# Dummy matmuls between the first transposes of a gated MLP kernel on one core

## The chip, the cores and the metric

The kernel runs on one core of a Trainium2 chip. The metric is the device time of one execution in microseconds (us). An execution that leaves a profile also has a span, from its first to its last instruction; the time is about 1.8 us more than the span (before: 544.01 us and 542.2 us for the same execution). Engines are called PE (matrix engine), DVE and ACT (vector and scalar), POOL, and SP, which issues transfers here.

## The reference

```python
# x: 2048 x 1024, w_gate and w_up: 1024 x 3584, w_down: 3584 x 1024, all bf16
g = einsum("bsd,df->bsf", x, w_gate)
u = einsum("bsd,df->bsf", x, w_up)
h = gelu_tanh(g) * u
return einsum("bsf,fd->bsd", h, w_down)
```

## The kernel before

The kernel is a tuned one; almost all of it is a dense stream of matmuls. Only its opening matters here. The first 512 rows of x arrive as four tiles of 128 rows. PE turns each tile by eight transposes (matmuls against an identity), DVE or ACT copies the result to SBUF, and then the first real matmuls run. Ahead of the transposes stand five dummy matmuls with zeros, to raise the clock of PE.

```python
NWARM = 5
...
warm = xpool.tile([P, N], bf16, name="warm")        # N = 512, P = 128
nc.vector.memset(warm, 0.0)
...
def turn(xT, xn, c, i, copy):                        # one row tile
    tp = bank[4 + i].bitcast(bf16).rearrange("p (k r) -> p k r", k=NKB)
    for ko in range(NKB):                            # NKB = 8
        nc.tensor.transpose(tp[:, ko, :], xn[i][:, ko * P : (ko + 1) * P], ident)
    copy(out=xT[c][:, :, i * P : (i + 1) * P], in_=tp)
...
xT = new_x()
xn0 = load_x(0)                                      # four transfers, x tiles 0 to 3
for k0, k1 in ((0, 2), (2, 5), (5, NKB)):
    load_wf(nc.sync, k0, k1)                         # first weight tile, gate and up
for ko in range(KH):
    transposing(xT, 1, ko, N)                        # second block of x
w = load_w(1)                                        # second weight tile, gate and up
...
for _ in range(NWARM):
    nc.tensor.matmul(bank[3], lhsT=warm[:, :P], rhs=warm, start=True, stop=True)
for i in range(NS):                                  # NS = 4
    turn(xT, xn0, 0, i, on_act if i == 1 else on_dve)
plain(bank[0:4], 0, range(0, 2), parts=2)            # 16 real matmuls of 256 columns
plain(bank[0:4], 0, range(2, NKB))                   # 24 of 512 columns
...
plain(bank[4:8], 1, range(KH))
...
nxt = {"p1": first_product(odd, xT, w)}              # needs the second weight tile
```

## Time and profile before

| | before |
|---|---|
| time, three executions | 542.15, 542.86, 543.13 us |
| the profiled execution: time, span | 544.01, 542.2 us |
| PE busy | 534.2 us, 99% of the span |
| half-rate stretch at the start | to about 10.3 us |

The first lines of the page, busy time and share of the span by engine:

```profile
span 542.2 us, 7385 instructions
## 1 busy us (share of the span) xinstructions
PE 534.2 (99%) x2371; PEld 379.3 (70%) x2405; DVE 341.0 (63%) x524; ACT 258.2 (48%) x463; POOL 238.9 (44%) x217
```

PE is the bound. The timeline of PE from 3 to 12 us, with start and length in us, the count after the x, and in brackets how long PE was idle before and what ended it:

```profile
2.44 1.06 PE L502 MATMUL bank<-warm 128*128 128x512 bf16 x2
3.63 1.89 PE L448 MATMUL bank<-ident,xn 128*128 128x128 bf16 x16
6.61 1.89 PE L448 MATMUL bank<-ident,xn 128*128 128x128 bf16 x16 [1.08 <-DMA xn<-in_x_dram]
8.29 3.96 PE L111 MATMUL bank<-xT,w 128*128 128x256 bf16 x20
```

Sixteen transposes take 1.89 us: one starts every 0.107 us. PE waits 1.08 us for x tile 2, and the first real matmul starts at 8.29 us. Narrower windows of the same timeline give the rate:

```profile
8.72 1.06 PE L111 MATMUL bank<-xT,w 128*128 128x256 bf16 x4
...
10.21 0.86 PE L111 MATMUL bank<-xT,w 128*128 128x256 bf16 x6
```

The last of a group adds its pipeline to the length: (1.06 - 0.42) / 3 = 0.213 us between starts at 9 us, where one such matmul has a length of 0.42. In the second row it is (0.86 - 0.27) / 5 = 0.118 us, with 0.27 the length of one there. So the clock doubles near 10.3 us. (The clock row of the page reads full speed from 0 on, because its first record begins at 10.28 us.)

The chain of waits of the first 25 us, start and length in us:

```profile
1.65 4.91 DMA xn<-in_x_dram
6.56 0.05 issue
6.61 1.89 PE bank L448 x16
8.50 2.68 PE bank L111 x16
11.17 0.05 issue
11.23 10.74 PE bank L111 x49
```

After the landing of x tile 2 the chain never leaves PE.

### The profile page before, as it was taken

What the parts mean: (1) busy time and instruction counts of PE and PEld (TensorE: products, weight loads), DVE (VectorE), ACT (ScalarE), POOL (GpSimd) and SP (SyncE); (2) the same over time, 40 slices, a digit from 0 to 9 for tenths busy, and PEclk for the clock granted to TensorE, in tenths of its full rate; (3) what the DMA queues carried; (4) which work ended last, traced back from release to release, by engine and by line L of the source; (5) the groups of instructions that cost most, each with busy time, mean ns of one, the idle gap of its engine ahead of it and who ended that gap; (6) DMA issues with size and microseconds to landing.
All of it is one profiled execution on the core that took longest, in us unless ns stands there. A gap on an engine that the chain in (4) does not pass through costs nothing.

```text
span 542.2 us, 7385 instructions
## 1 busy us (share of the span) xinstructions
PE 534.2 (99%) x2371; PEld 379.3 (70%) x2405; DVE 341.0 (63%) x524; ACT 258.2 (48%) x463; POOL 238.9 (44%) x217
## 2 busy tenths in 40 slices
PE   8999999999999999999999999999999999999997
PEld 5477777776776646888876677667777775488885
DVE  3796666667666894695945545555544459676730
ACT  2466666655666410165355555555555541114431
POOL 0169976667774500000097777777766600000000
PEclk9999999999999999999999999999999999999999
DMA  8976656667664899979763232232232069463751
GB/s 195 194 193 176 175 175 174 198 196 189 192 196 139 287 354 308 311 178 318 241 183 89 77 79 77 79 79 79 78 95 60 2 185 383 149 234 96 230 188 48
DMA packets 108133, 93.28 MB, mean 172 GB/s; under 512 B 17216, under 2 KB 92992, under 8 KB 108096
## 3 DMA queue, kind: packets, MB, share of 16 engines
q1 hardware_dynamic: 108096, 92.82, 59.3%
q8 instruction: 19, 0.31, 0.3%
q14 instruction: 18, 0.15, 0.1%
HBM read 74.45 MB, written 15.20 MB: 165 GB/s over the span
## 4 chain that ended last, share of the span: by engine, by line
PE 98%; DMA 1%; issue 0%; SPq 0%; ACT 0%
PE bank L111 97%; DMA xn<-in_x_dram 1%; PE bank L448 0%; SPq L441 0%; ACT st L412 0%
## 5 line engine op out<-in xcount | busy, mean ns | idle before, releaser
L93 POOL TENSOR_TENSOR s<-w 128x512 fp32r<-128x512 bf16 x102 | 119.2, 1188 | 155.3 <-PE bank L111 155.3
L111 PE MATMUL bank<-t,s 128*128 128x512 f32 x648 | 157.0, 398 | 0.0
L111 PEld LDWEIGHTS bank<-t,s 128*128 128x128 f32 x648 | 121.7, 188 | 27.7
L107 ACT COPY p<-bank 128x512 f32<-128x512 f32 x124 | 70.3, 590 | 98.0 <-PE bank L111 95.8
L111 PE MATMUL bank<-xT,w 128*128 128x512 bf16 (+1 forms) x476 | 111.4, 379 | 1.9
L90 DVE TENSOR_TENSOR hT<-g,bank 128x512 bf16<-128x512 f32 x112 | 76.7, 686 | 55.4 <-ACT g L179 49.9
L111 PEld LDWEIGHTS <-w 128*128 128x128 bf16 x504 | 45.7, 99 | 59.4 <-issue 13.5
L90 DVE TENSOR_TENSOR sum<-bank,p 128x512 f32<-128x512 f32 x54 | 37.3, 692 | 53.0 <-PE bank L111 50.8
L179 ACT ACTIVATE g<-sum 128x512 f32<-128x512 f32 x81 | 51.4, 634 | 33.6 <-DVE sum L90 32.6
L111 PE MATMUL bank<-q 128*128 128x512 f32 x240 | 58.9, 389 | 0.0
L111 PE MATMUL bank<-t,sa 128*128 128x512 f32 x216 | 58.6, 413 | 0.0
L93 POOL TENSOR_TENSOR s<-w,s 128x512 fp32r<-128x512 bf16 x50 | 57.7, 1172 | 0.0
L93 POOL TENSOR_TENSOR s<-s,w 128x512 fp32r<-128x512 f32 x50 | 57.0, 1161 | 0.0
L111 PE MATMUL bank<-tb,s 128*128 128x512 f32 x216 | 53.3, 389 | 0.0
L111 PEld LDWEIGHTS bank<-q 128*128 128x128 f32 x240 | 45.0, 188 | 9.4
L111 PE MATMUL bank<-raw,hT 128*128 128x512 bf16 x218 | 48.4, 379 | 0.3
L111 PEld LDWEIGHTS bank<-t,sa 128*128 128x128 f32 x216 | 40.7, 188 | 10.6
L111 PEld LDWEIGHTS bank<-tb,s 128*128 128x128 f32 x216 | 40.5, 188 | 8.4
L102 ACT CAST tb<-raw 128x512 fp32r<-128x512 bf16 x28 | 17.3, 626 | 60.6 <-DMA raw<-in_w_down_dram 28.5
L107 ACT COPY u<-bank 128x512 f32<-128x512 f32 x62 | 35.8, 589 | 17.9 <-PE bank L111 17.9
L90 DVE TENSOR_TENSOR bank<-bank,p 128x512 f32<-128x512 f32 x54 | 37.8, 699 | 8.5 <-PE bank L111 5.2
L90 DVE TENSOR_TENSOR q<-hT 128x512 fp32r<-128x512 bf16 x56 | 38.4, 686 | 4.2 <-PE bank L111 4.2
(45 smaller groups left out, 442.4 us busy)
## 6 DMA issues: line engine op xcount, KB each, us to landing
raw<-in_w_down_dram SPq DMA_DIRECT2D x80, 256.0 KB, 4.8
q<-td SPq DMA_DIRECT2D x60, 256.0 KB, 5.0
w<-in_w_gate_dram SPq DMA_DIRECT2D x27, 512.0 KB, 4.5
w<-in_w_up_dram SPq DMA_DIRECT2D x27, 512.0 KB, 6.3
td<-m SPq DMA_DIRECT2D x12, 768.0 KB, 4.5
w<-td SPq DMA_DIRECT2D x6, 1024.0 KB, 9.8
out_dram<-st SPq DMA_DIRECT2D x32, 128.0 KB, 1.7
td<-w SPq DMA_DIRECT2D x2, 768.0 KB, 7.1
```

Of the source, the lines that this page charges most:

```text
L90: nc.vector.tensor_tensor(out=out, in0=a, in1=b, op=op)
L93: nc.gpsimd.tensor_tensor(out=out, in0=a, in1=b, op=op)
L102: nc.scalar.copy(out=t, in_=src)
L107: nc.scalar.copy(out=t, in_=ps)
L111: nc.tensor.matmul(ps, lhsT=lhs, rhs=rhs, start=start, stop=stop, skip_group_check=True)
L179: nc.scalar.activation(g, src, ACT.Gelu_apprx_tanh)
```

## The change

The intent: keep PE busy between the transposes, so that its clock rises earlier. Three dummies of 256 columns go ahead of row tiles 1, 2 and 3.

```diff
-        for _ in range(NWARM):
-            nc.tensor.matmul(bank[3], lhsT=warm[:, :P], rhs=warm, start=True, stop=True)
+        def keep_warm(n, cols):
+            for _ in range(n):
+                nc.tensor.matmul(
+                    bank[3][:, :cols], lhsT=warm[:, :P], rhs=warm[:, :cols], start=True, stop=True
+                )
+
+        keep_warm(NWARM, N)
         for i in range(NS):
+            if i > 0:
+                keep_warm(3, 2 * P)
             turn(xT, xn0, 0, i, on_act if i == 1 else on_dve)
```

## The prediction

> **What bounds the kernel now.** TensorE. The profile's first part has PE busy 534.2 of 542.2 us; the chain that ended last lies to 97.4% on the matmul line. From 11.2 to 538.8 us PE never waits more than 0.07 us at a time. Only the first 11 us can improve.
>
> **The opening, from the timeline in narrow windows.** Five dummies run 1.19 to 3.50 us. Transposes of tiles 0 and 1 run 3.63 to 5.52, PE idles 1.08 us for tile 2 (landed 6.56), transposes of tiles 2 and 3 run 6.61 to 8.50, and the first real matmul starts at 8.29. Up to about 10.2 us the array runs at half rate: matmuls of 512, 256 and 128 columns start every 0.427, 0.213 and 0.107 us; from 10.3 us on every 0.216 (512) and 0.109 us (256). So the clock rises at about 10.3 us, and the real matmuls before it cost about 1 us too much. (The PEclk row, 1.0 all along, hides this.)
>
> The Trainium skill (TensorE: Matmul & The Clock Gate, Part 1) says that full rate is granted after about 3.4 us of sustained activity, in a free-running window. The trace agrees: a window ending at 10.28 would begin at 6.86, in unbroken work; the one before holds the idle microsecond. The same page (Part 4) says that transposes do not count as activity; here the full rate came after only 2 us of matmuls following transposes, so I think they count.
>
> **What the change adds.** Nine matmuls of 256 columns with zeros, three ahead of tiles 1, 2, 3: 0.64 us a group at half rate, 0.33 at full. Nothing else changes. The first two groups run while PE would wait for tile 2 anyway: tile 0 3.63-4.49, dummies to 5.13, tile 1 to 5.98, dummies to 6.62. Tile 2 starts on time at 6.62, without the gap. The third group, in front of tile 3, is on the critical path: +0.64 us at half rate.
>
> **Balance.** If the clock stays low, the first real matmul slips from 8.29 to about 8.97. But PE is now busy without a break from 3.63, so the clock should rise between 6.9 and 8.9 us. In the good case (about 6.9) tiles 2 and 3 finish near 8.0, the first matmuls wait for the up weights (landed 8.17), and the first block of x ends near 15.1 instead of 16.19 us. Then a next wait caps it: the up half of the second weight tile lands at 19.78 us, and its matmuls start at 20.5 now. So at most 0.7 us is kept against this profiled run. Its clock phase looks lucky, though: a full window after 6.6 us ends anywhere from 10.0 to 13.4, and each us costs 0.5. That would explain the spread of 542.15 to 543.13. Against the median the change then gains about 1 us. Later slack (DVE and POOL operands of the first unit are ready 1.4 to 2.6 us early) is enough not to give it back.
>
> **Prediction.** 541.9 us, 80% range 541.1 to 542.9. Faster by over 2%: 0.2%; within 2%: 99.5%; slower: 0.3%.
>
> **What would show it.** No PE gap before tile 2's transposes; 256-column matmuls at 0.109 us from the first real one, or nearly; the first real matmul at 8.0 to 8.5 us; a new PE wait of up to 1 us near 19 us for the up weights; PE without waits after it; span 541.3 to 541.9.
>
> **What would make it wrong.** Zeros or transposes not counting as activity: then the clock still rises near 10.3 us, the first real matmul is at 8.97 and the kernel is 0.3 us slower. Or the weights landing later than in the profile; or a run-to-run spread larger than the effect.

## The result, and the profile after

The changed kernel takes 542.37 us (median of 4 executions, 542.12 to 542.51), the kernel before 542.50 (4 executions, 541.78 to 543.13). The ratio is 0.9997, with a 95% interval from 0.998 to 1.0015: the same. Ratios here are not quite the ratios of the medians quoted.

The two profiles, however, differ by 1.7 us. The first lines of the page after:

```profile
span 540.5 us, 7403 instructions
## 1 busy us (share of the span) xinstructions
PE 533.0 (99%) x2380; PEld 378.3 (70%) x2414; DVE 340.8 (63%) x524; ACT 258.3 (48%) x463; POOL 238.9 (44%) x217
```

The timeline of PE after, 3 to 12 us:

```profile
3.53 0.91 PE L448 MATMUL bank<-ident,xn 128*128 128x128 bf16 x8
4.27 0.49 PE L503 MATMUL bank<-warm 128*128 128x256 bf16 x3
4.60 0.61 PE L448 MATMUL bank<-ident,xn 128*128 128x128 bf16 x8
5.05 0.49 PE L503 MATMUL bank<-warm 128*128 128x256 bf16 x3
6.25 0.62 PE L448 MATMUL bank<-ident,xn 128*128 128x128 bf16 x8 [0.71 <-DMA xn<-in_x_dram]
6.71 0.49 PE L503 MATMUL bank<-warm 128*128 128x256 bf16 x3
7.03 0.61 PE L448 MATMUL bank<-ident,xn 128*128 128x128 bf16 x8
7.48 4.87 PE L111 MATMUL bank<-xT,w 128*128 128x256 bf16 x28
```

The three dummies of the first group already run at full rate ((0.49 - 0.27) / 2 = 0.11 us apart); the first clock record begins at 4.17 us. **The clock rose before the first of the new dummies began, at 4.27 us.** They cannot have caused it, and the difference between the two profiles is no measure of the change. The chain of waits after shows the rest of it, the earlier landing of x tile 2 (6.20 instead of 6.56 us) and the shorter matmuls:

```profile
1.65 4.55 DMA xn<-in_x_dram
6.20 0.05 issue
6.25 0.62 PE bank L448 x8
6.87 0.33 PE bank L503 x3
7.20 0.45 PE bank L448 x8
7.64 1.90 PE bank L111 x16
```

One more reading from the traces: from the first fp32 matmul (26.36 us before, 24.73 after) to the end it is 515.84 and 515.80 us. In the nine further profiles of real kernels below it is 515.67 to 515.96 us. So what separates these kernels happens in the opening, to within 0.3 us, and is kept to the end.

### The profile page after: what moved, and what is told of

The parts are those of the page before. It is cut to its first block, busy times and chain, and to the rows that moved or that the text cites. A ratio compares the mean times of both kernels' runs of the same rounds, so it can differ in the third digit from the quotient of the medians.

```text
span 540.5 us, 7403 instructions
## 1 busy us (share of the span) xinstructions
PE 533.0 (99%) x2380; PEld 378.3 (70%) x2414; DVE 340.8 (63%) x524; ACT 258.3 (48%) x463; POOL 238.9 (44%) x217
## 4 chain that ended last, share of the span: by engine, by line
PE 98%; DMA 1%; issue 0%; SPq 0%; ACT 0%
PE bank L111 98%; DMA xn<-in_x_dram 1%; PE bank L448 0%; SPq L441 0%; ACT st L412 0%; PE bank L503 0%
## 5 line engine op out<-in xcount | busy, mean ns | idle before, releaser
L111 PEld LDWEIGHTS <-w 128*128 128x128 bf16 x504 | 45.1, 98 | 59.1 <-issue 13.4
```

Source lines behind the costliest of these rows:

```text
L111: nc.tensor.matmul(ps, lhsT=lhs, rhs=rhs, start=start, stop=stop, skip_group_check=True)
```

## The experiments

The prediction takes the clock to be decided anew at the end of every window of about 3.4 us; where these windows lie in the kernel (their phase) changes from execution to execution. **Theory "gap"**: idle time while PE waits for x spoils the window in which the clock could rise; the dummies fill it. **Rival "phase"**: only the position of the free-running window decides, and the dummies do nothing.

### e1: many openings in one execution

The clock's window has some phase in each execution, and one profile shows one phase. So 72 openings were put in front of the unchanged kernel, each with its own loads and preceded by an idle stretch that the DVE makes by a long memset. The core of the edit, condensed:

```diff
+def opening(rep, nwarm, groups, only_transposes=False):
+    nc.vector.tensor_copy(out=rseen, in_=bank[3][:, :1])      # waits for PE
+    nc.vector.memset(flat[:, : 18000 + 542 * rep], 0.0)       # idle stretch for PE
+    ... two columns of each x and weight tile, then `warm`, set by DVE: releases loads and dummies
+    ... loads of x and of the first weight tile as in the kernel; dummies(nwarm, 512)
+    for i in range(NS):
+        if i > 0: dummies(groups[i - 1], 256)
+        turn(rx, rxn, 0, i, ...)
+    ... the 40 real matmuls of the first block
+KINDS = [(5, (0,0,0)), (5, (3,3,3)), (5, (3,3,0)), (6, (3,3,0)), (0, (0,0,0)), (0, (0,0,0), True)]
```

> 72 openings in one execution, ahead of the unchanged kernel (the output stays right, the time is meaningless). Each is preceded by 9 to 16 us without work for the tensor engine, so each meets the clock's window at another phase. Six kinds in turn, 12 of each: B as before (5 dummies, no groups), A as after (groups 3,3,3), A2 without the third group (3,3,0), F with a sixth first dummy (6; 3,3,0), N without any dummies, X without dummies but with 72 further transposes of the first tile. GAP theory (the clock rises at the end of the first 3.4 us window that is busy for some share between 62% and 80%; the idle microsecond spoils it for some phases, the dummies fill it): counted from the first dummy, B rises in two groups, about half of its openings at 2.7 to 4.6 us and about half at 8.0 to 9.5 us; A and A2 all at 2.7 to 6.1 us; the opening of A is then shorter than B's by 0.3 to 0.8 us in the mean, by 1.3 to 1.7 us in the phases where B is late and by nothing in the others. PHASE theory (the dummies do nothing, the two profiles only met other phases): B and A have the same mix of early and late rises. X: if transposes count as activity the rise comes while they still run, 2.7 to 6.8 us after the first; if not, only after the matmuls behind them have run for 2 us or more. A minus A2: 0 to 0.15 us, for the weights hide the third group.

Measured, from the release of the first dummy to the start of the last matmul of the first block, and how often the clock rose later than 7 us after that release:

```
kind                 n  mean   lowest-highest  late rises
B  (before)         12  13.58  12.23 - 15.10   4   (9.11 to 9.57 us; mean of these 14.83, of the others 12.95)
A  (after)          12  13.14  12.31 - 13.86   0
A2 (third gone)     12  13.10  12.67 - 13.70   0
F  (sixth, 3,3,0)   12  13.13  12.62 - 13.67   0
N  (no dummies)     12  13.69  13.07 - 15.22   9   (8 of these 7.25 to 7.95, one 10.30)
```

B has late rises and A has none. By itself this does not refute the phase theory, for the phases were not spread evenly: in ten of the 12 B openings the first dummy came 0.73 to 1.19 us into a window of the clock, in A only once near there (1.21 us; otherwise at 0.47 to 0.63 and at 2.41 to 2.57). e5 mends this. The gap theory is right only in part: late rises are a third and not half (the means differ by 0.44 us, within the foretold 0.3 to 0.8), six of B's eight early rises came at 5.75 to 6.02 us, where 2.7 to 4.6 had been foretold, and B when it is early is 0.19 us *faster* than A. Two openings of kind B at the same phase (the window begins 0.91 us before the release of the first dummy) show that the phase alone does not decide, and what does. Windows of 3.41 us on the clock's grid: PE busy with count, granted clock, DMA share, GB/s. First the late one:

```profile
763.59:767.00 3.41, 2.41 (x23) 0.50 0.95 292
767.01:770.42 3.41, 3.41 (x24) 0.50 0.59 165
```

Then the early one:

```profile
913.78:917.19 3.41, 2.91 (x28) 0.50 1.02 316
917.19:920.60 3.41, 3.41 (x30) 1.00 0.55 142
```

And their timelines, late first:

```profile
763.62 1.70 PE L448 MATMUL bank<-ident,xn 128*128 128x128 bf16 x14
766.32 1.89 PE L448 MATMUL bank<-ident,xn 128*128 128x128 bf16 x16 [1.00 <-DMA xn<-in_x_dram]
```

```profile
913.62 1.89 PE L448 MATMUL bank<-ident,xn 128*128 128x128 bf16 x16
916.00 1.62 PE L448 MATMUL bank<-ident,xn 128*128 128x128 bf16 x16 [0.50 <-DMA xn<-in_x_dram]
```

The first of these windows decides: with a wait of 1.00 us it was busy for 2.41 of 3.41 us and the clock stayed; with 0.50 us it was busy for 2.91 and the clock rose. A wait for x costs the clock its rise only when it takes too much of a window.

The clock changes lie on one grid through the whole execution: every stretch at one rate within the openings is 10.24, 13.65 or 17.07 us long, three, four or five times 3.413. I worked out the busy share of each window from the starts of the matmuls (columns over the rate, transposes and zeros counted). Of 138 windows at half rate with any work, the 72 that raised the clock had shares of 0.755 and more; those that did not had 0.763 and less, so the two sets part at about 0.76, with an overlap of 0.008. That is theory **"share"**: a window raises the clock when PE was busy for about 0.76 of it; some 0.8 us of waiting (0.24 of 3.41) does not cost the rise.

Kind X answers whether transposes count. Windows before and after the rise of one opening in which PE had done nothing but transposes:

```profile
135.54:138.95 3.41, 3.41 (x34) 0.50 1.04 322
138.96:142.37 3.41, 3.41 (x64) 1.00 0.54 142
```

```profile
135.27 5.92 PE L506 MATMUL bank<-ident,xn 128*128 128x128 bf16 x72 [13.83 <-DMA xn<-in_x_dram]
```

The rise at 138.95 us lies amid the transposes, and before them PE was idle for 13.8 us. In all 12 openings of X it came 5.57 to 7.26 us after the release, while the first other matmul ran at 10.18 us or later. Transposes count. (Counted from the first transpose, as foretold, it came after 3.06 to 4.88 us, inside the 2.7 to 6.8. In A and A2 the rise was to come at 6.1 us at the latest, and the latest came at 6.31 and 6.33. A minus A2 is 0.04 us, inside the 0 to 0.15, but the two met different phases, so this hardly tells it from nothing.)

### e2, e3, e4: the real kernels again

e2 is the kernel before, e3 the changed one, both without an edit; e4 is before without its five dummies:

```diff
-    NWARM = 5
+    NWARM = 0
```

> The kernel before against itself, as the measure of noise: ratio 1.000. GAP theory: its executions fall into an early and a late kind, about 1.3 to 1.7 us apart (near 541.9 and near 543.5 us). PHASE theory says the same of before, so this run only sets the scale.

> The changed kernel on the same chip. GAP theory: all executions in the early kind, spread under 0.6 us, median 0.2 to 0.8 us below that of before depending on how many of the before executions are late. PHASE theory: the same two kinds and the same spread as before, medians within 0.3 us either way.

> Before without its first five dummies. Both theories: nearly always a late rise (at 9.3 us or later), so all executions in the late kind or later, 543.3 to 545 us; this gives the whole cost of a late clock in the real kernel, 1.3 to 2.5 us over the early kind. If it is no slower than before, the rise of the clock is not what separates the kinds.

Measured: e2 541.92 us (541.68 to 542.15, 5 executions), all early, ratio 0.9995; e3 542.46 (541.69 to 542.81), ratio 1.0004; e4 542.61 (542.24 to 542.71), ratio 1.0005. The nine executions of before beside them: 541.93 to 542.51, and one of 543.74. So before did show a late kind, but rarely here, and the changed kernel was not faster; its spread of 1.1 us is also wider than foretold. e4 is a miss: I expected 543.3 to 545. In its profile x tile 2 landed at 5.31 us, the window from 5.28 to 8.70 us was busy for 0.98, and the clock rose at 8.70 us; so no dummies at all cost only about 0.1 us against before (542.50 and 542.38 in the mean). By my own words, that a kernel no slower than before would mean that the rise of the clock does not separate the kinds, this counts against the theory as I had it. In this profile the clock rose 2.77 us later than in that of e2 (8.70 and 5.93 us), but the first fp32 matmul came only 0.39 us later (24.95 and 24.56). In the first profile of before, where x tile 2 was late too, it came 1.80 us later than in e2. So the late kind is not the late clock alone.

The profile of e2 shows how small the wait can be. PE, 3 to 8 us:

```profile
3.50 2.81 PE L448 MATMUL bank<-ident,xn 128*128 128x128 bf16 x24
6.50 0.62 PE L448 MATMUL bank<-ident,xn 128*128 128x128 bf16 x8 [0.18 <-DMA xn<-in_x_dram]
```

Here x tile 2 landed at 5.46 us; the waits for tiles 2 and 3 were 0.11 us (merged into the first row) and 0.18 us. The 1.08 us of the first profile was an unusual landing.

### e5: the share theory, with evenly spread phases

The same rig (edit condensed) with a randomly drawn idle stretch, and five kinds, 18 openings each. S has seven first dummies and no groups; BL and AL load the first weight pair ahead of x tiles 2 and 3, so that these land later.

```diff
-nc.vector.memset(flat[:, : 18000 + 542 * rep], 0.0)
+nc.vector.memset(flat[:, : 18000 + 2 * rand.randrange(3277)], 0.0)
+KINDS = [(5,(0,0,0)), (5,(3,3,3)), (7,(0,0,0)), (5,(0,0,0),True), (5,(3,3,3),True)]   # True: late x
```

> 90 openings in one execution ahead of the unchanged kernel, 18 of each of five kinds, with a randomly drawn idle stretch before each, so that the phases of the clock's windows spread evenly: B (5 dummies; no groups), A (5; groups 3,3,3), S (7; no groups), and BL and AL, which are B and A with the first weight pair loaded ahead of x tiles 2 and 3, so that these land about 0.9 us later. SHARE theory, from the first rig: a window of 3.41 us raises the clock when the array was busy for about 0.755 of it or more, transposes and zeros included; so idle time under 0.83 us in a window does no harm, and dummies cost their own time where x has landed already. It expects no window over 0.77 without a rise and none under 0.74 with one. Times to the last matmul of the first block, counted from the release of the first dummy: B and A equal in the mean within 0.2 us (worked out 13.2 each), S shorter than both by 0.1 to 0.2; A's spread smaller than B's. BL late in about 40% of its openings, AL in none, AL shorter in the mean by 0.7 to 1.1 us. Rival PHASE theory: B and A, and BL and AL, have the same share of late rises and AL is not shorter than BL. Rival GAP theory as it was foretold for the first rig, that any idle wait spoils a window: then B would be late in 40% of its openings too, and A shorter than B by 0.5 us or more.

```
kind              n   mean   lowest-highest  late rises  clock fell again
B  (before)      18   13.38  12.35 - 14.73   6           0    (mean of the late 14.38, of the others 12.89)
A  (after)       18   13.15  12.60 - 13.71   0           0
S  (seven)       18   13.07  12.23 - 13.44   0           0
BL (before,late) 18   15.49  13.81 - 17.68   8           9
AL (after, late) 18   14.21  13.49 - 15.26   0           0
```

Of 189 windows at half rate with any work none under 0.771 raised the clock and none over 0.745 failed to: the rule held as foretold. The phases now spread: of the ten B openings with the first dummy 0.9 to 2.7 us into a window six were late, of the ten A openings there none, and so the phase theory is refuted.

A is 0.26 us slower than an early B (13.15 and 12.89) and 1.23 us faster than a late one: the change is an insurance with a premium. Part of the 0.26 is not the dummies' doing, for B is early where x lands early: x tile 2 landed 4.50 us after the release in these openings, 4.97 in the late ones, 4.67 in A. Counted from the landing of the first up weights, the mean is 6.78 us in A, 6.60 in early B and 6.59 in S, which leaves 0.18. It lies in the nine openings of A whose clock rose after 4.3 us: there the first matmul with up weights began 0.44 us behind their landing, in the other nine 0.05, in early B 0.09. (These landings were worked out from the trace afterwards.)

B minus A is 0.23, just over the 0.2 that I allowed; S is 0.31 shorter than B and 0.08 than A, where 0.1 to 0.2 had been foretold.

With a late x the gain is 1.28 us, above the foretold 0.7 to 1.1: eight of 18 BL openings rose late, near the foretold 40%, but in nine others the clock had risen and fell again. One of these, on the grid:

```profile
212.31:215.72 3.41, 3.30 (x18) 0.50 0.75 220
215.73:219.13 3.40, 1.20 (x18) 1.00 1.05 326
219.14:222.55 3.41, 3.41 (x22) 0.50 0.28 68
```

A window at full rate with 1.20 of 3.40 us of work cost the next window its rate. Over both rigs the clock fell after shares up to 0.391 and was kept from 0.374 on.

### e6, e7: the real kernel with a late x

```diff
-    xn0 = load_x(0)
-    for k0, k1 in ((0, 2), (2, 5), (5, NKB)):
+    xn0 = load_x(0, range(0, 2))
+    load_wf(nc.sync, 0, 2)
+    xn0 += load_x(0, range(2, NS))
+    for k0, k1 in ((2, 5), (5, NKB)):
         load_wf(nc.sync, k0, k1)
```

e6 is this on the kernel before, e7 on the changed one (load_x there takes the rows).

> The kernel before with the first weight pair loaded ahead of x tiles 2 and 3, so that the array always waits about 1 us or more for tile 2. SHARE theory: about 40% of the executions late; mean 0.8 to 1.6 us above the kernel before (near 543.5 us), spread up to 1.7 us. PHASE theory: only the later landing shows, 0.5 to 0.9 us.

> The same with the dummies of the change. SHARE theory: none late, mean 0.5 to 1.2 us below the late-x kernel without them (near 542.7), spread under 0.7 us. PHASE theory: equal to that kernel, or slower by up to 0.3 us.

Measured: e6 544.63 us (542.67 to 546.67, 6 executions), e7 542.98 (542.49 to 543.59, 6). The means, 544.74 and 542.98, lie 1.8 us apart, more than the foretold 0.5 to 1.2, and the changed kernel's spread is 1.1 us against 4.0. (Foretold were spreads under 0.7 and up to 1.7; and e6 lies 2.0 us above before beside it, not 0.8 to 1.6.) Where waits are long, the dummies do what they were meant to do. The profile of e6 shows the cost, PE by windows of the grid and its timeline:

```profile
0.78:4.19 3.41, 3.00 (x14) 1.00 0.72 212
4.19:7.61 3.42, 1.24 (x18) 1.00 0.99 247
7.61:11.02 3.41, 2.38 (x16) 0.50 1.27 212
11.02:14.43 3.41, 3.41 (x14) 0.50 0.60 110
```

```profile
6.78 0.62 PE L448 MATMUL bank<-ident,xn 128*128 128x128 bf16 x8 [1.97 <-DMA xn<-in_x_dram]
8.64 1.03 PE L448 MATMUL bank<-ident,xn 128*128 128x128 bf16 x8 [1.24 <-DMA xn<-in_x_dram]
```

The clock rose at 4.19 us (the first row's 1.00 stands there only because no record covers it), fell at 7.61 after a window with 1.24 us of work, and came back at 14.43 us. In e7 the window from 5.07 to 8.48 us was busy for 0.70 and the rate was kept.

### e8 to e11: a cheaper form, and a wait behind it

e8 and e10 are the kernel before with `NWARM = 7` and no groups. I meant them to fill the wait ahead of tile 0, where nothing has landed that could be held up. That is not quite so: in e8 tile 0 landed at 3.46 us and its transposes began at 4.15. The wait for tile 2 takes up most of this delay: its transposes began 0.28 us after the landing in e8 (5.86 and 5.58) and 0.05 in e10 (5.62 and 5.57). e9 is the changed kernel once more. e11 is e10 with the second weight tile loaded in halves:

```diff
-    w = load_w(1)
+    w = load_w(1, cuts=((0, KH), (KH, NKB)))    # gate and up of the first half, then of the second
```

> The kernel before with two more first dummies (7 of 512 columns, no groups), a candidate that beats both: SHARE theory: the wait before tile 0 is filled, so that a window can hold the wait for tile 2 and still count 0.755; mean 0.1 to 0.2 us below both kernels and spread under 0.6 us, which the timing can hardly tell from nothing. PHASE theory: slower than before by 0 to 0.3 us.

> The changed kernel once more, beside many executions of before, to count the two kinds. SHARE theory: before again shows a late kind (543 us and more) in about 3 of 10 executions and an early kind near 542.0; the change shows no late kind and lies near 542.3, about 0.3 above the early kind of before, for its dummies sometimes hold up x tiles that have landed; the means differ by less than 0.3 us. A theory in which the change gives a real gain would have it below the early kind of before, under 542.0.

> Seven first dummies, no groups, once more. SHARE theory: no late kind, and 0.0 to 0.2 us below the changed kernel on the same chip (near 542.2), as nothing stands between an x tile that has landed and its transposes.

> Seven first dummies, and the second weight tile loaded in halves so that the half which the first products need comes first. In two profiles with an early start (before again, seven dummies) the array waited 0.19 and 0.46 us near 19 us for the up half of this tile. If that wait caps the gain, the wait is gone and the time is 0.1 to 0.5 us below seven dummies (near 541.9). If the stretch after it is bound by DVE or POOL operands that come no earlier, or the smaller transfers cost as much, the time is the same as e10's within 0.1 us.

| run | median us | lowest to highest | mean of the run, of before beside it | ratio, 95% interval |
|---|---|---|---|---|
| e8 seven | 542.29 | 541.67 to 542.97 | 542.34, 542.75 | 0.9991, 0.9974 to 1.0008 |
| e9 after | 542.40 | 542.11 to 542.75 | 542.39, 542.45 | 0.9999, 0.9985 to 1.0012 |
| e10 seven | 542.02 | 541.79 to 542.54 | 542.16, 542.45 | 0.9995, 0.9982 to 1.0007 |
| e11 seven, split | 542.07 | 541.54 to 542.36 | 541.95, 542.45 | 0.9990, 0.9978 to 1.0003 |

Beside e8 the kernel before showed its two kinds openly: six executions from 541.66 to 542.51 and five from 543.53 to 543.96. Beside e9 it had two of nine above 542.8, not three of ten above 543. The spread of e8, 1.3 us, is wider than the foretold 0.6.

The profile of e10 shows more. PE from 0 to 8 us, first two rows:

```profile
1.19 3.04 PE L502 MATMUL bank<-warm 128*128 128x512 bf16 x7 [1.19 <-DVE warm L432]
4.07 1.06 PE L448 MATMUL bank<-ident,xn 128*128 128x128 bf16 x16
```

The first clock record begins at 3.98 us, and the transposes from 4.07 us on start every 0.056 us, at full rate. Until then PE had run nothing but dummies with zeros: zeros count.

The wait that e11 was to remove, in the profile of e8:

```profile
19.08 3.20 PE L111 MATMUL bank<-xT,w 128*128 128x512 bf16 x14 [0.46 <-DMA w<-in_w_up_dram]
```

In the profile of e11 PE works through that stretch without a wait:

```profile
14.64 7.72 PE L111 MATMUL bank<-xT,w 128*128 128x512 bf16 x35
```

There the needed up half landed at 16.73 us, instead of the whole up tile at 19.03 in e8. But e10, without the split, did not wait there either: its up tile landed at 18.39 us. So e10 against e11 is no test of that wait. In the mean e11 is 0.5 us below before and 0.4 below the changed kernel; its interval against before still holds 1, and e10 to e11 is 0.2 us of mean with equal medians. It is the fastest version tried, but the times alone don't prove it.

## Why the prediction was right or wrong

The time, 542.37 us, lies in the range, and "same" was given 99.5%. The path to it was in part wrong.

- **Right:** PE is the bound, and the first 11 us are the only place. Half rate to 10.3 us. Transposes count as activity (e1, kind X). The clock's windows of about 3.4 us run freely (one grid in e1). The dummies do remove the late kind: in the rigs A has none in 30 openings and B ten, and all 38 executions of before against all 14 of the changed kernel agree with it.

```
                          n    mean    lowest - highest
before, all              38   542.45   541.66 - 543.96
  up to 542.81           28   542.09   541.66 - 542.51
  above 542.81           10   543.46   542.82 - 543.96
after, all               14   542.36   541.69 - 542.81
```

  The cut at 542.81 is mine, the slowest execution of the changed kernel. Ten of 38 times a saving of 543.46 - 542.09 = 1.37 us is 0.36 us in the mean; the changed kernel lies 542.36 - 542.09 = 0.27 us above the early kind. The rest is 0.09 us, 542.45 - 542.36, and it does not bear weight. Eleven of the 38 were taken beside e5 to e8, where five were late and the changed kernel itself was not run; without them before has 542.33 us in the mean (27 executions, five above 542.81), 0.02 *below* the changed kernel. Nor does the timing alone prove that the late kind is gone: that the ten highest of 52 all fall to before has a chance of 3% if the kernels were the same, and that the five highest of 41 do, without those eleven, 11%. The rig of e5 gives a premium of the same size, 0.26 us, with the part of early landings in it.

- **Wrong, the balance: "Its clock phase looks lucky" and "Against the median the change then gains about 1 us".** The profiled execution of before took 544.01 us, longer than each of the 38 timed ones. It was unlucky in its phase (the clock rose 9.1 us after the first dummy; late rises in the rigs came after 7.6 to 9.6) and in x tile 2, which landed at 6.56 us (5.31 to 6.20 in the eight other profiles of the real kernel in which x is loaded first). The gain in the mean is 0.09 us in the whole pool, none without the eleven beside e5 to e8, and not 1, because most executions of before lose nothing.

- **The step that failed: that full work is needed, "a full window after 6.6 us ends anywhere from 10.0 to 13.4".** A window needs about 0.76 of work. The windows of e2 (0.85 of work from 2.52 to 5.93 us) and of most B openings pass with their waits, so the clock of before usually rises without help, in both rigs then within 6.3 us of the release of the first dummy.

- **Mis-sized: "The first two groups run while PE would wait for tile 2 anyway".** That rests on the wait of 1.08 us. With the waits of e2, 0.11 and 0.18 us, the two groups at half rate (6 x 0.213 = 1.28 us) hold up tiles that have landed. That is the likely source of the premium, for in e5 it lies in the openings whose clock rose after 4.3 us, not in those where it rose earlier; A against early B shows the sum, not each group by itself. Of the signs foretold, the missing gap before tile 2 failed: in the profile after, with the groups at full rate, PE still waited 0.71 us.

- **Mis-sized: the third group "is on the critical path: +0.64 us at half rate".** Taking it away was worth 0.04 us (A2 against A in e1, which met different phases), no more than the rig can tell from nothing. In the profile after, the real matmuls begin at 7.48 us, but the third needs the up weights, which landed at 7.80 us, and starts at 7.84.

- **Partly right: the wait for the second up weights near 19 us.** It appeared in e2 (0.19 us; the up tile landed at 18.65 us) and e8 (0.46; 19.03), not in the three profiles of the changed kernel (18.00 to 18.65) and not in e10, which opens faster than all of these (18.39).

- The span I named, 541.3 to 541.9, ignored that the span is 1.8 us shorter than the time; 540.5 was measured.

The Trainium skill was a good guide to the mechanism, without the share that a window needs. TensorE: Matmul & The Clock Gate, Part 1, describes a free-running window of 3413 ns, and the grid of 3.413 us in e1 agrees. It also says that "the ramp penalty is <1% of a typical kernel span; don't fit to a specific cold count"; here the late kind costs 1.37 of 542 us, 0.25%.

What stays open: how much each of the two first groups costs, and whether e11 is truly faster than the kernels before and after. No execution of the late kind among the 38 left a profile; that they are late for the same reasons as the first profile and the rigs is inferred from their times. The weights and x landed up to a microsecond apart from one execution to the next; why was not tried.

## What to carry to other kernels

One profile of a short opening shows one phase of the clock and one order of landings; before a gain is drawn from it, look at the spread of the times, and repeat the opening many times in one execution if the clock matters. Keep-busy work is an insurance: put it where a later wait takes up what it delays (here ahead of the first tile), and only as much as the window needs. Where waits for data are long, as in e6, it is worth having, also because a clock that has risen can fall again.

## What the Trainium skill lacked or had wrong

- TensorE: Matmul & The Clock Gate, Part 1, gives no busy share that a window needs. In e5 windows at 0.745 and less did not raise the clock and windows at 0.771 and more did; in e1 the border was 0.755 to 0.763.
- The same page, "Why this matters for your kernels", in its row on throughput drops, advises no PE-idle gaps over about 3 us and names one window of idle as the cause of a fall. In e6 the clock fell at 7.61 us after a window with 1.24 us of work, in which no wait was longer than 1.97 us; in the rigs it fell after shares up to 0.391 and was kept from 0.374 on.
- The same page, Part 4, says that full rate doesn't engage for transposes and that they don't count as PE-busy the same way. In e1 the clock rose amid transposes alone in all 12 openings of kind X, and 64 of them then ran in a window that had held 34.
- No page that I read says whether matmuls with zeros count. They do: in e10 the window that raised the clock at 3.98 us was busy for 0.82, all of it dummies with zeros, and in the profile after the window that raised it at 4.17 us was busy for 0.80, of which five dummies with zeros made up 0.62.
